# A second Strassen level for output product 4, with the sums behind h split at the chunk boundary

## The chip, the core and the metric

The kernel runs on one core of a Trainium2 chip. A core has a matrix engine (TensorE, PE in the profile; its weight loads are listed as PEld), a vector engine (VectorE, DVE), a scalar engine (ScalarE, ACT), a general engine (GpSimd, POOL) and SyncE (SP), which here only issues DMAs. Each engine works through its own instructions in order and waits on semaphores where it needs another engine. Matmul results land in PSUM, which has eight banks of 2 KB per partition; everything else lives in SBUF. The metric is the device time of one execution in microseconds (us). It is a little longer than the span of the profile, which runs from the first to the last instruction.

## The reference

All data are float32. A linear attention feeds a two-layer network:

```python
def _attn_ref(q, k, v, g_norm):            # (8, 8, 576, 64) each
    kv = np.einsum('bhsd,bhse->bhde', k, v)
    out = np.einsum('bhsd,bhde->bhse', q, kv)
    rms = np.sqrt(np.mean(out * out, axis=-1, keepdims=True) + 1e-06)
    return (out / rms * g_norm).astype(np.float32)

def _moe_ref(x, w_in, w_out):              # (4608, 512), (512, 2048), (2048, 512)
    h = x @ w_in
    g = np.maximum(0.01 * h, h)
    return (g @ w_out).astype(np.float32)
```

The attention's output is turned to (4608, 512) before it goes into the network. The two products of the network are nearly all of the arithmetic.

## The kernel before

**Blocks and chunks.** The 4608 rows are nine blocks of 512 (`NB`), the 2048 hidden columns four chunks of 512 (`NC`). Block 0 is computed plainly while the weights arrive. Blocks 1 to 8 use the Strassen-Winograd scheme: a product of 2x2 blocks from seven products instead of eight, at the price of sums of operands and of results. The products are numbered 1 to 7 and run in the order 1, 2, 6, 5, 7, 3, 4 (`ORDER`). In what follows h1 means product 1 of the hidden layer, o4 product 4 of the output. The output chunks are counted through as n = 4 (block - 1) + chunk, from 0 to 31.

**The hidden product.** From block 2 on h is computed by two levels (`product_h_two`, L930): each outer product holds seven inner ones of 128 columns each. Outer group k runs 7 matmuls in two PSUM banks, four in one and three in the other (`ha` and `hb`, or `hc` and `hd`). ACT copies the first results of a quadrant to `qa` and `qc` in SBUF, and DVE adds the later ones. At the end of a chunk seven DVE adds of 512 columns each turn `qa` and `qc` into g's four quadrants (L959 to 967), ACT applies the leaky ReLU (`relu`), and POOL forms the four operand sums of the output product (`sums_of`). h4 of the chunk is the last before that; h1 of the next chunk overwrites the first part of `qa` and `qc`.

**The output product.** `product_o` (L973) runs one product per slot, each four matmuls of 256 columns into a bank `oa` or `oc`. A chunk has seven slots, t = 0 to 6; in each, PE does one group of h and then one output product of an earlier chunk. o1 of chunk n begins in slot 2 of the following chunk. A bank keeps accumulating: 1, 6, 7, 4 in one, 2 in the other, then 5 and 3 in that other one again. After each product DVE (ACT for the first writing of a block) adds the bank into one of four output tiles, named `11`, `12`, `21`, `22`. From chunk 4 on product 2 is itself done by a second level: its seven matmuls of 128 columns use the fourth column group that the three-product bank of h leaves empty (`Second`, L905); there the order is 1, 5, 6, none, 7, 3, 4. Its operand sums of g come from POOL (`inner_g`, L893), 128 columns each.

**Right-hand sides.** The sums of w_out's blocks are formed once, in block 1, by POOL (`sides_w2`), written to DRAM, and from then on loaded by SP for each chunk into `t12` (products 5 and 6) and `t34` (products 7 and 4), 512 KB each. w_in's 49 pieces per chunk are read group by group into a ring of five (`read`, `RING`).

**Order.** From block 2 on the order on each engine is the program's (`pin`). The loop near the end of the function places attention work of the next batch (`FINE_SLOTS`, `LATE_SLOTS`) and the x sums of the next block (`sides_x`, slots 20 to 22, with POOL's `inner` in slots 24, 25 and after 27) into the slots, counted 0 to 27 within a block.

Of the kernel before, what the change touches and what calls it, by code (L numbers as in the profile page):

```python
# [23 lines left out]
def kernel(  # L24
# [77 lines left out]
    pairs = consts.tile([P, 4 * NW], F32, name="pairs")  # L102
# [85 lines left out]
    ident = consts.tile([P, P], F32, name="ident")  # L188
# [470 lines left out]
    t12, t34 = pair(2, 2, U, N2), pair(3, 2, U, N2)  # L659
    writes = []  # L660

    def sides_w2(n):
# [7 lines left out]
        def sums(i):  # L670
            t = (t12, t34)[i]
            if n >= NC:
                pin(nc.sync.dma_start(t, w2_dram[c][i]))
                return
# [73 lines left out]
    xt24 = [work.tile([P, 2, 2, N2], F32, tag="xt24", name="xt24"),  # L748
# [3 lines left out]
    def sides_x(i):  # L752
# [7 lines left out]
        if i == 1:  # L760
            t4 = opool.tile([P, 2, N2], F32, tag="o", name="xt4", bufs=6)
# [22 lines left out]
        def inner(kind):  # L784
            for y11, y12, y21, y22, t1, t2, t4 in batches:
# [10 lines left out]
    def strassen(tags, left, right, done, order=ORDER, pieces=None):  # L796
# [4 lines left out]
        for i in order:  # L801
# [21 lines left out]
            for part in range(2):  # L823
                for r in range(2):
                    matmul(bank[:, part, :], lhsT=left(i, part, r), rhs=right(i, part, r),
                           start=i in FRESH and part == 0 and r == 0, stop=(r == 1),
                           skip_group_check=True)
            done(i, bank.rearrange("p u (v n) -> p (u v) n", v=2))
            yield

    def relu(t, src=None):
        nc.scalar.activation(t, t if src is None else src, func=AF.Prelu, alpha=SLOPE)  # L832
# [48 lines left out]
    gi = view(pairs, 12 * P, 4, P)  # L881
# [11 lines left out]
    def inner_g(c, half):  # L893

        g = g_of(c)[3]
        a11, a21, a12, a22 = (g[:, n, :] for n in range(4))
        s1, s2, s3, s4 = (gi[:, n, :] for n in range(4))
# [31 lines left out]

    def product_h_two(i, c, quarters, to, second):  # L930
# [5 lines left out]
        banks = {}  # L936
        for t, k in enumerate(ORDER):
            for js, tags, q in zip(GROUPS, (("ha", "hc"), ("hb", "hd")), (qa, qc)):
# [11 lines left out]
                if fresh:  # L950
                    nc.scalar.copy(q[:, at], bank)  # L951
                else:
                    add(nc.vector, q[:, at], bank, q[:, at])
# [4 lines left out]
        g11, g21, g22, g12 = g_of(c)  # L958
        add(nc.vector, g21, qa[:, :, 0, :], qa[:, :, 1, :])  # L959
        add(nc.vector, g11, qa[:, :, 0, :], qc[:, :, 0, :])  # L960
        yield
        add(nc.vector, g22, g21, qa[:, :, 2, :])
        add(nc.vector, g12, g22, qa[:, :, 3, :])
        yield
        add(nc.vector, g22, g22, qc[:, :, 1, :])
        yield
        add(nc.vector, g21, g21, qc[:, :, 1, :])
        add(nc.vector, g21, g21, qc[:, :, 2, :])
        for t in (g11, g12, g22, g21):
            relu(t)  # L970
        sums_of(c, to)

    def product_o(n, g_sides, os, finish, second):  # L973
# [3 lines left out]
        sums = sides_w2(n + 1)[1] if n + 1 < NC * (NB - 1) else lambda i: None  # L977
        if c == 0:

            for key in ("12", "22", "11", "21"):  # L980
                os[key] = opool.tile([P, 2, N2], F32, tag="o", name=f"o{key}", bufs=6)

# [6 lines left out]
        def done(i, bank):  # L989
            key, fresh = into[i]  # L990
            if isinstance(bank, list):
# [13 lines left out]
            if c == NC - 1 and i in (2, 7, 3, 4):  # L1005
                finish(key, os[key])

            if i == (6 if second else 5):
                sums(0)
            elif i == 4:  # L1010
                sums(1)


        yield from strassen((("oa", "oc"), ("oc", "oa"))[n % 2], lambda i, part, r: g_sides[i][:, 2 * r + part, :],
                            lambda i, part, r: w_sides[i][:, r, :], done,
                           (1, 5, 6, None, 7, 3, 4) if second else ORDER,
                           pieces=pieces)
# [19 lines left out]
    def first_block(between):  # L1037
# [28 lines left out]
        for t in range(4):  # L1066
            o = opool.tile([P, DM], F32, tag="o", name="o", bufs=6)
# [47 lines left out]
    LATE_SLOTS = (3, 4)  # L1115

# [6 lines left out]
    seconds = {}  # L1123
# [12 lines left out]
    for i in range(1, NB):  # L1136
# [4 lines left out]
        for c in range(NC):  # L1141
# [3 lines left out]
            for t in range(7):  # L1145
                slot = 7 * c + t
                go(h_steps, 1)
                if not one:

                    if t == 6:  # L1150
                        go(h_steps, 1)
                    if slot in LATE_SLOTS:
# [102 lines left out]
```

## Time and profile before

| what | value |
|---|---|
| median of 3 runs | 917.1 us (916.8 to 918.18) |
| the profiled execution's own time | 917.21 us |
| its span | 915.5 us |
| granted TensorE clock | 1.00 |
| POOL, four sums of g per output chunk (128x512) | 1277 to 1376 ns each |
| POOL, operand sum of product 2 (128x128) | 456 to 510 ns each |
| DVE, add of an output bank (128x512) | 683 ns |
| DVE, add of a product-2 result (128x128) | 286 ns |
| DVE, add for g (128x512) | 684 to 692 ns |
| SP, load of t12 or t34 (512 KB) | 4.3 us from issue to landing |

A row of the profile gives a source line, an engine, an operation, the tile written and the tiles read, shapes, a count, busy time, the mean duration and the idle time before it with what ended it. Many rows have one helper's line: L118 is the matmul helper and L636 the add helper, so tiles tell them apart. A float32 matmul shows as two records. Durations of matmuls overlap, so their cost is read from start to start.

### The profile page before, as it was taken

The page shows a single profiled execution, that of the slowest core. Times are in us where ns is not written, and L with a number is a line of the kernel's source. Part 1 is how long each engine was busy: PE and PEld are TensorE (multiplying, and loading weights), DVE is VectorE, ACT ScalarE, POOL GpSimd, SP SyncE. Part 2 cuts the span into 40 slices and gives each one's busy share as a digit, 9 for nine tenths or more (in the row PEclk, how much of TensorE's full clock was granted, in tenths as well). Part 3 has the DMA queues.
Part 4 walks back from the last instruction along what each step waited for, and adds up shares of the span by engine and source line. Part 5 has one row for each costly group of instructions (what it writes and reads, how often), then busy time and mean ns, then how long its engine had stood idle before and what let it go on. Part 6 is the DMA issues. An engine that isn't in the chain of part 4 may idle for free.

```text
span 915.5 us, 18030 instructions
## 1 busy us (share of the span) xinstructions
PE 909.1 (99%) x6976; PEld 775.6 (85%) x6976; DVE 628.2 (69%) x1168; ACT 327.6 (36%) x645; POOL 367.0 (40%) x440
## 2 busy tenths in 40 slices
PE   8999999999999999999999999999999999999998
PEld 5444448888998999899999999999999999999997
DVE  5876985587457876587756786678659755755565
ACT  5454533242135233533343324332343333223330
POOL 2000246977633472226321642264226422642222
DMA  9999908895599678877896689658765676667632
GB/s 267 243 243 237 239 35 258 263 304 167 175 360 286 224 213 263 235 233 211 255 261 216 219 250 263 230 179 227 224 184 176 188 221 200 184 187 223 199 107 92
DMA packets 90229, 200.06 MB, mean 219 GB/s; under 512 B 9888, under 2 KB 42272, under 8 KB 90144
## 3 DMA queue, kind: packets, MB, share of 16 engines
q1 hardware_dynamic: 79680, 187.04, 69.5%
q10 hardware_dynamic: 10016, 10.69, 3.4%
q8 instruction: 56, 0.92, 0.4%
q0 software_dynamic: 448, 1.18, 0.3%
q14 instruction: 29, 0.24, 0.1%
HBM read 172.39 MB, written 26.48 MB: 217 GB/s over the span
## 4 chain that ended last, share of the span: by engine, by line
PE 95%; DMA 2%; DVE 1%; POOL 1%; issue 0%; ACT 0%; ACTq 0%; DVEq 0%; POOLq 0%
PE o_a L118 18%; PE o_c L118 18%; PE h_ha L118 11%; PE h_hb L118 11%; PE h_hc L118 8%; PE h_hd L118 8%; PE o_acc L118 6%; PE h_ps L118 6%; PE o_ps L118 3%; PE h_a L118 1%; PE h_c L118 1%; PE kv_ps L118 1%; DMA pairs<-in_v_dram 1%; PE h_b L118 1%; PE h_d L118 1%; DMA w<-pairs 1%
## 5 line engine op out<-in xcount | busy, mean ns | idle before, releaser
L636 POOL TENSOR_TENSOR gs<-g 128x512 f32<-128x512 f32 x64 | 81.7, 1277 | 253.3 <-ACT g L832 253.3
L832 ACT ACTIVATE g<-g 128x512 f32<-128x512 f32 x124 | 78.2, 631 | 130.4 <-DVE g L636 130.4
L951 ACT COPY w_all<-h_ha 128x512 f32<-128x512 f32 x84 | 48.9, 582 | 173.9 <-PE h_ha L118 160.5
L118 PE MATMUL o_a<-pairs,gs 128*128 128x256 f32 x384 | 91.3, 381 | 0.0
L118 PE MATMUL o_c<-pairs,gs 128*128 128x256 f32 x376 | 89.2, 380 | 0.0
L636 DVE TENSOR_TENSOR o<-h_hb,o 128x128 f32<-128x128 f32 x104 | 29.8, 286 | 83.3 <-ACT pairs L951 83.2
L118 PEld LDWEIGHTS o_a<-pairs,gs 128*128 128x128 f32 x384 | 69.8, 190 | 9.2 <-POOL pairs L636 1.2
L636 DVE TENSOR_TENSOR o<-o_c,o 128x512 f32<-128x512 f32 (+1 forms) x91 | 61.1, 672 | 24.1 <-PE o_c L118 23.7
L118 PEld LDWEIGHTS o_c<-pairs,gs 128*128 128x128 f32 x376 | 68.3, 190 | 7.6
L636 DVE TENSOR_TENSOR o<-o_a,o 128x512 f32<-128x512 f32 x75 | 51.2, 682 | 28.2 <-PE o_a L118 28.1
L118 PE MATMUL h_ha<-stage,w_all 128*128 128x128 f32 x448 | 59.6, 276 | 0.0
L118 PEld LDWEIGHTS h_ha<-stage,w_all 128*128 128x128 f32 x448 | 56.6, 192 | 3.0 <-issue 0.7
L118 PE MATMUL h_ps<-xT,w_all 128*128 128x512 f32 (+1 forms) x136 | 58.1, 571 | 0.3 <-DVE w_all L258 0.3
L118 PE MATMUL o_acc<-w,g 128*128 128x512 f32 x128 | 57.7, 594 | 0.0
L636 DVE TENSOR_TENSOR g<-g,pairs 128x512 f32<-128x512 f32 x84 | 55.6, 689 | 1.9
L636 POOL TENSOR_TENSOR pairs<-g 128x128 f32<-128x128 f32 x52 | 23.7, 456 | 77.3 <-PE h_hb L118 48.5
L118 PEld LDWEIGHTS h_ps<-xT,w_all 128*128 128x128 f32 x136 | 25.4, 190 | 29.0 <-issue 26.1
L118 PEld LDWEIGHTS o_acc<-w,g 128*128 128x128 f32 x128 | 24.1, 190 | 30.2 <-issue 29.9
L636 DVE TENSOR_TENSOR w_all<-h_hc,w_all 128x512 f32<-128x512 f32 x56 | 38.3, 684 | 15.9 <-PE h_hc L118 15.6
L636 DVE TENSOR_TENSOR o<-h_hd,o 128x128 f32<-128x128 f32 x78 | 22.0, 283 | 38.2 <-ACT pairs L951 38.1
L118 PE MATMUL h_hb<-stage,w_all 128*128 128x128 f32 x336 | 46.7, 275 | 0.0
L636 POOL TENSOR_TENSOR pairs<-w 128x512 f32<-128x512 f32 x4 | 5.3, 1328 | 98.7 <-ACT cut L245 98.7
(229 smaller groups left out, 2262.4 us busy)
## 6 DMA issues: line engine op xcount, KB each, us to landing
w_all<-w SPq DMA_DIRECT2D x196, 448.0 KB, 4.2
pairs<-w SPq DMA_DIRECT2D x56, 512.0 KB, 4.3
out_dram<-o ACTq DMA_DIRECT2D x35, 256.0 KB, 4.4
v_in<-in_v_dram SPq DMA_DIRECT2D x29, 288.0 KB, 5.5
k_in<-in_k_dram SPq DMA_DIRECT2D x28, 288.0 KB, 5.3
q_in<-in_q_dram SPq DMA_DIRECT2D x56, 144.0 KB, 6.0
q_in<-in_q_dram SPq DMA_DIRECT2D x56, 140.0 KB, 6.0
w<-stage SPq DMA_DIRECT2D x12, 512.0 KB, 4.8
```

The costliest lines, as they stand in the source:

```text
L118: pin(nc.tensor.matmul(*args, **kw))
L636: ins = eng.tensor_tensor(out_, a, b_, op=ALU.subtract if minus else ALU.add)
L832: nc.scalar.activation(t, t if src is None else src, func=AF.Prelu, alpha=SLOPE)
L951: nc.scalar.copy(q[:, at], bank)
```

## The change

For the 21 chunks n = 8 to 28, product 4 is taken out of the sequence and done by two levels in a bank of its own use: seven matmuls of 128 columns in four steps, in slots 1 to 4 of the chunk after the one in which o1 ran (step 1 directly behind o1 of the next chunk). The bank is the one that held products 1, 6 and 7, after it was read. Its results go into tile `21` as seven parts of 128 columns. The sum of products 1, 6 and 7, which product 4 used to be added to, now goes into a tile `7` of its own, which is added to `22` and `21` once per block. The order of the other products becomes 1, none, 6, 5, 7, 3, none.

The operands: POOL's `inner_g` forms its sums for two quadrants of g at once (256 columns). Seven right-hand pieces per chunk are formed on POOL in block 2, written to DRAM by POOL's DMA queue (`w4_dram`), and loaded by SP from block 3 on (`f4` and `f4_more`); the load of `t34` is split accordingly.

The seven adds for g are split: first all seven for the quadrant that the next h1 overwrites (128 columns), then the rest (384 columns), two at once, two at the end of the chunk, and three after the next chunk's h1. The ReLUs, the copies of h and the sums of g follow in program order. The x sums move from slots 20 to 22 to slots 22, 24 and 25, POOL's `inner` parts are spread over slots 24, 25, 26 and the next block's slot 0. Output tiles are taken when first written, from four buffers and two for `11`, where there were six; `ident` moves into the home of `xt24`.

```diff
-    pairs = consts.tile([P, 4 * NW], F32, name="pairs")
+    pairs = consts.tile([P, 4 * NW + 4 * P], F32, name="pairs")
...
+    w4_dram = [dram.tile([P, 7, P], F32, name=f"w4_{c}") for c in range(NC)]
+    t12, t34 = pair(2, 2, U, N2), view(pairs, 28 * P, 2, U, N2)
+    f4 = t34[:, 1].rearrange("p u (v n) -> p (u v) n", v=2)
+    f4_more = view(stage, 21 * P, 3, P)
+
+    def four(n):
+        return 2 * NC <= n < NC * (NB - 1) - 3
...
+            if n >= NC and i:
+                if row != 1:
+                    pin(nc.sync.dma_start(t[:, 0], w2_dram[c][i][:, 0]))
+                if row == 0:
+                    return
+                if not four(n):
+                    pin(nc.sync.dma_start(t[:, 1], w2_dram[c][i][:, 1]))
+                    return
+                pin(nc.sync.dma_start(f4, w4_dram[c][:, :4, :]))
+                pin(nc.sync.dma_start(f4_more, w4_dram[c][:, 4:, :]))
+                return
...
-        a11, a21, a12, a22 = (g[:, n, :] for n in range(4))
-        s1, s2, s3, s4 = (gi[:, n, :] for n in range(4))
+        a11, a21, a12, a22 = (g[:, n, 2:, :] for n in range(4))
+        s1, s2, s3, s4 = (gi_two[:, :, n * P:n * P + P] for n in range(4))
...
+    class Fourth:
+        STEPS = (1, 2, 5), (6, 3), (7,), (4,)
+        COLUMN = {1: 0, 6: 0, 7: 0, 4: 0, 2: 1, 5: 2, 3: 2}
...
+        def step(self, at):
+            if at == 0:
+                self.bank = ps_m.tile([P, 4, P], F32, tag=self.tag, name=f"f_{self.tag}")
+            for k in self.STEPS[at]:
+                matmul(self.bank[:, self.COLUMN[k], :], lhsT=self.left[k], rhs=self.right[k],
+                       start=(k == 1), stop=True, skip_group_check=True)
+            for k in self.STEPS[at]:
+                bank = self.bank[:, self.COLUMN[k], :]
+                v, s = INTO[k]
+                to = self.o_of("21")[:, v, s * P:s * P + P]
+                if self.n % NC == 0 and k in (1, 5, 6, 4):
+                    nc.scalar.copy(to, bank)
+                else:
+                    add(nc.vector, to, bank, to)
+            if at == 3:
+                self.last()
...
+        for _ in add_up(0, 1):
+            pass
+        for _ in add_up(1, 4):
+            yield
         yield
-        for t in (g11, g12, g22, g21):
-            relu(t)
+        for g in g_of(c):
+            pin(relu(g))
         sums_of(c, to)
...
+            if fourth and i == 7:
+                if c == NC - 1 or not four(n + 1):
+                    add(nc.vector, os["22"], os["22"], os["7"])
+                if c == NC - 1:
+                    finish("22", os["22"])
...
+            elif i == 4 and NC <= n < 2 * NC:
+                inner_w4()
+                pin(nc.gpsimd.dma_start(w4_dram[c][:, :4, :], f4))
+                pin(nc.gpsimd.dma_start(w4_dram[c][:, 4:, :], f4_more))
+                later.append([3, lambda: sums(1, 1)])
...
+        def last():
+            sums(1, 1)
+            if c == NC - 1 or not four(n + 1):
+                add(nc.vector, os["21"], os["21"], os["7"])
+            if c == NC - 1:
+                finish("21", os["21"])
+        order = ORDER
+        if fourth or four(n - 1):
+            order = (1, None, 6, 5, 7, 3, None if fourth else 4)
...
+    FOURTH_AT = {1: 0, 3: 2, 4: 3}
...
+                    if t == 0:
+                        go(h_rest)
+                    if slot == 0 and inner_rest:
+                        inner_rest(2)
+                    if t in FOURTH_AT and four((i - 1) * NC + c - 2):
+                        fourths[(i - 1) * NC + c - 2].step(FOURTH_AT[t])
...
-                        if slot in (20, 21, 22):
-                            go(sums, 2 if slot == 20 else 1)
+                        if slot in (22, 24, 25):
+                            go(sums, 2 if slot == 24 else 1)
                         if slot == 24:
-                            inner(0)
+                            inner(0, (1, 3))
                         elif slot == 25:
-                            inner(1)
+                            inner(0, (0,))
+                            inner(1, (0, 3))
+                        elif slot == 26:
+                            inner(0, (2,))
+                            inner(1, (1, 2))
...
-            go(h_steps)
+            if one or (i, c) == (NB - 1, NC - 1):
+                go(h_steps)
+            else:
+                go(h_steps, 1)
+                h_rest = h_steps
```

`add_up(lo, hi)` holds the seven adds of before for the quadrants lo to hi; `inner_w4` forms the three sums and the difference of the right-hand pieces by four POOL instructions of 128 columns.

## The prediction

> **What bounds the kernel now.** I read the page's busy shares first, then the chain of waits, then the wait list of the tensor engine alone, then the table of stretches for one block of 512 rows, and last the timelines of each engine around one chunk.
>
> ```profile
> PE 909.1 (99%) x6976; PEld 775.6 (85%) x6976; DVE 628.2 (69%) x1168; ACT 327.6 (36%) x645; POOL 367.0 (40%) x440
> ...
> PE 95%; DMA 2%; DVE 1%; POOL 1%; issue 0%; ACT 0%; ACTq 0%; DVEq 0%; POOLq 0%
> ```
>
> The wait list of PE (who waited, on whom, us in total, times, longest), and the stretch of one block (its length, then busy us and instructions of PE, PEld, DVE, ACT and POOL, clock, DMA share, GB/s):
>
> ```profile
> PE idle_ps L118 <- DVE group L294: 1.5, 1, 1.5
> PE kv_ps L118 <- DMA pairs<-in_v_dram: 0.8, 1, 0.8
> ...
> 446.17:543.05 96.88, 96.88 (x849) 89.86 (x848) 69.72 (x135) 35.51 (x72) 38.12 (x48) 1.00 0.79 237
> ```
>
> To be seen: TensorE (PE) is the bound, 95% of the chain. Its two longest waits, 1.5 and 0.8 us, lie in the start. In the block from 446.17 to 543.05 it is busy for all 96.88 us at full clock, while VectorE (DVE) is busy 72%, ScalarE (ACT) 37%, GpSimd (POOL) 39% and the DMA engines 79%. So time falls only with PE's own work, and rises only where PE starts to wait. What a product costs is read from PE's timeline (start, us, engine, line, operation, tiles, count):
>
> ```profile
> 513.16 1.89 PE L118 MATMUL o_a<-pairs,gs 128*128 128x256 f32 x8
> 514.89 0.38 PE L118 MATMUL h_hc<-xT,w_all 128*128 128x128 f32 x2
> ...
> 516.67 1.06 PE L118 MATMUL h_ha<-stage,w_all 128*128 128x128 f32 x8
> ```
>
> From start to start, four matmuls of 256 columns (each is two records) take 514.89 - 513.16 = 1.73 us. The next eight of 128 columns take 516.67 - 514.89 = 1.78 us, 0.2225 each. The durations beside them overlap and are not used.
>
> **What the Trainium skill says.** "SBUF — State Buffer", section "Who interferes with whom": a DVE instruction with two SBUF inputs and a GpSimd instruction that reads SBUF take the same port, and the second blocks for the other's whole length. The trace agrees: DVE's x subtraction takes 0.68 us with POOL idle and 1.28 us beside one of POOL's sums:
>
> ```profile
> 495.55 0.68 DVE L636 TENSOR_TENSOR w_all<-xT 128x512 f32<-128x512 f32 x1
> 502.27 1.28 DVE L636 TENSOR_TENSOR xT<-xT 128x512 f32<-128x512 f32 x1
> ...
> 501.74 1.26 POOL L636 TENSOR_TENSOR gs<-g 128x512 f32<-128x512 f32 x1 [9.38 <-ACT g L832]
> 503.08 1.62 POOL L636 TENSOR_TENSOR gs<-gs,g 128x512 f32<-128x512 f32 x1
> ```
>
> "PSUM — Partial Sum Buffer", section "PSUM bank collisions raise a hardware error": two engines on one bank must be ordered, readers too. Here that shows as DVE's 128x128 add waiting for ACT's copy from the same bank:
>
> ```profile
> 532.71 0.48 ACT L951 COPY pairs<-h_hd 128x384 f32<-128x384 f32 x1 [0.31 <-PE h_hd L118]
> ...
> 533.22 0.29 DVE L636 TENSOR_TENSOR o<-h_hd,o 128x128 f32<-128x128 f32 x1 [1.29 <-ACT pairs L951]
> ```
>
> "DMA: Bandwidth & Descriptors", section "Anatomy of one DMA — SWDGE (gpsimd) path", prices a GpSimd DMA at 2.0 us plus bytes at 436 GB/s: about 2.6 us for 256 KB. The trace shows such DMAs only in the crowded start.
>
> **The change part by part.** The clock of one chunk, from its first h matmul, in us of PE time: h1 0, o3 of the chunk before 1.78, h2 3.51, step 0 of the new product 5.29, h6 5.96, o1 7.74, step 1 9.47, h5 9.91, step 2 11.69, h7 11.92, step 3 13.70, o6 13.92, h3 15.65, o5 17.43, h4 19.16, o7 20.94, end 22.67. A tile is readable about 0.25 us after its last issue (ACT's copies start 0.3 us after it).
>
> 1. Matmuls. 21 chunks (n = 8 to 28) replace 1.73 us by 7 x 0.2225 = 1.56 us: 0.17 each, 21 x 0.1725 = 3.6 us off PE. It is all on the path. The built order has 147 of the new matmuls, 21 x 7, and no other PE work changes.
>
> 2. Evacuation. One add of 512 (next one starts 0.60 after) becomes seven of 128 (0.20 apart, 0.29 where one needs the other). Splitting g turns 7 adds into 7 of 128 and 7 of 384 (0.47 apart): 7 x 0.68 against 7 x 0.60, +0.6. About +1.6 us of DVE per chunk of 22.7, in a lane with some 6 us free: no cost in total, only where a column is needed back. Steps 0 to 3 reuse column 0, so each waits for the evacuation before it. Tightest is step 2 to step 3: h5 is readable at 11.94, ACT's copy ends at 12.45, the 128x128 add of the same bank follows, then step 2's own add, done at about 13.05; step 3 wants it at 13.70. Spare 0.65. The cover is h7; without it every chunk would stall by over 1 us.
>
> 3. g split. DVE's quadrant adds run from -0.8 to 1.0, the rest from 1.0 to 5.3; ACT's relus now stand behind h1's copies and end near 7; POOL's s1 starts at 6.5 and s2 ends at 9.1. o1 (7.74) needs only g11, o6 (13.92) needs s2: spare over 4. h6 needs h1's bank back: before that copy came at +4.4 (499.52), now at 2.5. No cost.
>
> 4. POOL. Four operand sums double from 128 to 256 columns (456 to about 750 ns, from the 128x256 rows): +1.2 us per chunk, POOL about 45% busy. But in the last chunk of a block the inner x sums now wait for x terms that DVE makes at about 17.6 (they moved from slots 20 to 22 to slots 22, 24, 25). After that POOL still has some 8.7 us of work (twelve sums, 0.46 to 0.76 each) and ends about 2 us inside the next chunk; before, it ended at 518.57, ahead of g's adds. There the quadrant adds share its port: a 128x128 SBUF add beside POOL is 548 ns in the block-1 rows, so 7 of them take about 3.1 us and not 1.8. With the two 1.25 us q transposes of slots 1 and 2 (1.08 apart) ahead, step 1's evacuation ends near 12.0; step 2 wants it at 11.69. Stall about 0.3, at the start of blocks 4, 5 and 6 (later ones have no q left): 0.9 us. Bounds: 0 if POOL ends early, 0.6 each if DVE loses the port throughout.
>
> 5. Last chunk of a block. With attention, x terms and step 3's add, DVE frees step 3's bank at about 19.1; o5 wants it at 19.6 (PE has 2.2 us of attention there). Spare 0.2 to 0.5 in five blocks. I take 0.1 in all, bounds 0 and 1.5.
>
> 6. DMA. Per chunk 256 KB become 448 KB: 21 x 192 KB, 4 MB on 200. Loads go out at 13.9 and are used 14 us later; they land in 4.3 us. SP holds them until step 3 is done, and behind them stand the reads of w1's ring, each free 17 us ahead: nothing. In block 2 POOL forms the sums (4 x 0.46) and writes them out by its own queue four times. Write, wait and reload must fit in seven slots, about 24.7 us: POOL is done at 13.7, the write lands by 17 (skill's price) to 22 (8 us, the start's POOL rows), the reload 4.3 later, before 28.1. Only the third write has 2.7 us more POOL work before it and could be late. Bounds 0 and 2 us; I take 0.
>
> 7. Moved homes (ident, output tiles) and ACT's copies at a block's first chunk: all released a chunk or more before use, nothing. The three last chunks keep the old product; g11's relu comes by 894, o1 wants it at 900.06: nothing.
>
> Sum on the profiled execution's 917.2 us (span 915.5): -3.6 + 0.9 + 0.1 = -2.6, so 914.6. It lies 0.1 above the median of 917.1, which changes nothing. Beyond 0.2% (1.8 us, what a measurement can tell from no change): under 915.3 is faster, over 918.9 slower.
>
> **The rivals.**
> - B, the gain is mostly eaten. For: the port and the bank of points 4 and 5, with spares below 0.5 us that come from a schedule added up by hand. Against: each occurs once per block. Price: 3 x 0.6 + 5 x 0.2 = 2.8 plus some of point 6: -0.8 or so, 916.4.
> - C, slower: the column 0 chain in step 1 to step 3. If one attention operation of 1.1 to 1.25 us stands ahead of an evacuation on DVE or ACT in each of the 14 chunks that carry attention (10 to 23), the evacuation is 1.2 late, the spare 0.65 is gone and PE waits 0.6: 14 x 0.6 = 8.4, less 3.6 is +4.8, 922. It decides for slower from 5.4 / 14 = 0.39 us a chunk, that is, from 1.04 us later than in point 2. Against: in the built order these operations stand behind step 2's add, except in the first chunk (point 4).
> - That the change does nothing is ruled out by the 147 matmuls; more than 3.6 us cannot come, as PE has no waits to lose in the loop.
>
> **How the numbers follow.** Likeliest, A: 914.6, own range 913.4 (all of 3.6, no stall) to 915.3, chance 0.65. B, 0.22, from 915.3 to 918.9. C, 0.13. The range 913.4 to 917.6 leaves out C and the upper end of B. Faster 0.65, same 0.22, slower 0.13.
>
> **What would show it.** Right: 147 matmuls f<- of 0.22 us start to start; the chunk on PE shorter by 0.17; in PE's wait list at most single waits of 0.3 us on DVE, at blocks 4 to 6's first chunks; POOL busy up to 2 us past a block's start. Wrong: f or o matmuls waiting for DVE in most chunks (C), or for a DMA in the second block (point 6).

## The result, and the profile after

| kernel | median | runs | lowest to highest |
|---|---|---|---|
| before | 916.72 us | 6 | 916.44 to 918.18 |
| changed | 921.25 us | 6 | 920.52 to 923.01 |

The ratio is 1.0049, 95% interval [1.0037, 1.0062]: slower by 4.5 us, where 914.6 was forecast, with a range from 913.4 to 917.6. The profiled execution of the changed kernel took 920.52 us with a span of 918.8, so 3.3 us over the profile before. It is the fastest of its six.

The page, busy time of the engines and the chain of waits:

```profile
PE 908.7 (99%) x7102; PEld 776.6 (85%) x7102; DVE 678.7 (74%) x1478; ACT 330.1 (36%) x669; POOL 417.9 (45%) x464
...
PE 88%; DVE 5%; POOL 3%; DMA 2%; issue 1%; ACT 1%; DVEq 0%; ACTq 0%; SPq 0%; POOLq 0%
```

PE has 126 records more and 0.4 us less busy time. The forecast's 3.6 cannot be read there, as the page counts a stall as busy in part (block 5's first chunk: 23.40 of 23.93 us busy, with some 1.2 of stall). PE's share of the chain fell from 95% to 88%, and DVE and POOL took 5% and 3%. PE's wait list (us in total, times, longest):

```profile
PE idle_ps L118 <- DVE group L295: 1.5, 1, 1.5
PE o_a L118 <- issue: 1.4, 1, 1.4
PE f_oa L118 <- DVE o L637: 1.2, 3, 0.4
PE o_c L118 <- DVE o L637: 0.8, 1, 0.8
PE h_ha L118 <- ACT w_all L1029: 0.5, 1, 0.5
```

The first wait is the old one of the start. The other four are new. The `f_oa` row is the forecast's own sign, three waits of 0.4 at three blocks' starts. The `o_a`, `o_c` and `h_ha` rows were not forecast. The stretch of the block that was shown before, from and to the same h1:

```profile
448.06:545.52 97.46, 96.93 (x873) 90.11 (x872) 77.78 (x185) 36.02 (x76) 44.26 (x48) 1.00 0.77 243
```

It has become longer, 97.46 for 96.88 us, and PE is no longer busy in all of it. The whole difference lies in a few chunks. A chunk is written here as the block whose rows h is computed for, and its place in it. Lengths from h1 to h1, read from PE's timeline of the two kernels, in us:

| chunk | before | changed | difference |
|---|---|---|---|
| all others from n = 10 on, for instance block 5's third | 25.19 | 25.02 | -0.16 to -0.17 each |
| block 2's last, block 3's first | 24.27, 22.86 | 24.40, 24.59 | +0.13, +1.73 |
| block 4's, 5's, 6's first | 22.87, 22.86, 22.87 | 23.88, 23.93, 24.09 | +1.01, +1.07, +1.22 |
| block 6's last | 24.08 | 24.54 | +0.46 |
| block 7's, 8's first | 22.87, 22.87 | 23.02, 22.88 | +0.15, +0.01 |
| block 7's last | 23.26 | 22.70 | -0.56 |
| last h4 to the end | 27.6 | 28.6 | +1.0 |

With 0.165 us saved in each of 21 chunks, the matmuls give 3.5 us, as forecast. Against them stand stalls of 1.86 us (block 3), 3.80 (blocks 4 to 6: the difference and 0.165, each), 0.48 (blocks 7 and 8), 0.63 (block 6's end) and 1.0 (tail), less 0.40 for a stall of the kernel before in block 7 that is gone. The sum is +3.9; the profiled start was 0.65 us shorter, which makes the 3.3.

**Where a block begins.** DVE, POOL and PE of the changed kernel around h1 of block 5 (521.59), from the timeline:

```profile
521.07 0.72 POOL L637 TENSOR_TENSOR w_all<-w_all 128x256 f32<-128x256 f32 x1
521.66 0.28 DVE L637 TENSOR_TENSOR g<-w_all 128x128 f32<-128x128 f32 x1
521.75 0.77 POOL L637 TENSOR_TENSOR pairs<-g 128x256 f32<-128x256 f32 x1
521.87 0.81 DVE L637 TENSOR_TENSOR g<-w_all,pairs 128x128 f32<-128x128 f32 x1
522.49 0.78 POOL L637 TENSOR_TENSOR pairs<-g,pairs 128x256 f32<-128x256 f32 x1
522.60 1.14 DVE L637 TENSOR_TENSOR g<-g,w_all 128x128 f32<-128x128 f32 x2
523.77 0.82 DVE L637 TENSOR_TENSOR g<-g,pairs 128x128 f32<-128x128 f32 x3
...
528.83 0.68 DVE L637 TENSOR_TENSOR o<-o_c,o 128x512 f32<-128x512 f32 x1
529.12 0.39 PE L118 MATMUL h_hb<-w,pairs 128*128 128x128 f32 x2
529.66 1.97 PE L118 MATMUL o_c<-w,g 128*128 128x256 f32 x8
...
532.70 1.23 DVE L456 STREAM_TRANSPOSE qT<-q_in 128x576 f32<-128x576 f32 x1
533.77 0.60 DVE L637 TENSOR_TENSOR o<-f_oa,o 128x128 f32<-128x128 f32 x2
534.43 0.49 PE L118 MATMUL f_oa<-stage,pairs 128*128 128x128 f32 x2 [0.39 <-DVE o L637]
```

The seven quadrant adds run from 521.66 to 524.51, 2.85 us. In the tail, where POOL is idle, the same seven take 1.79 (892.95 to 894.74). Until POOL ends at 523.27, one 128x128 add occupies up to 0.81 us and not 0.28. All that DVE does next is late. o3's evacuation ends at 529.51 and lets o1 into its bank at 529.66, while h6 had been issued by 529.34 (529.12 and 0.22). These 0.32 us cost 0.57 in all, as o1 takes 1.89 us to the next start and not 1.73, and the first matmul of step 1 0.32 and not 0.22. Step 1's two adds, behind a q transpose, end at 534.37; step 2 follows, 0.55 us late, at a cost of 0.66. The two make the 1.24 us of this chunk.

The adds that are lengthened have both inputs in SBUF. A DVE add of a PSUM bank is not: in block 2's last chunk, at 319.53, one of 128x512 takes 0.68 us beside POOL's 128x128 sum from 319.56, which takes 0.46.

In block 3 it is worse, as POOL also forms block 2's `inner_w2` sums:

```profile
327.40 1.55 DVE L637 TENSOR_TENSOR g<-g,w_all 128x128 f32<-128x128 f32 x2
328.98 1.70 DVE L637 TENSOR_TENSOR g<-g,pairs 128x128 f32<-128x128 f32 x3
...
330.96 0.76 POOL L637 TENSOR_TENSOR w<-w,w 128x128 f32<-128x128 f32 x1
332.06 0.68 DVE L637 TENSOR_TENSOR o<-o_a,o 128x512 f32<-128x512 f32 x1
332.84 1.97 PE L118 MATMUL o_a<-pairs,g 128*128 128x256 f32 x8 [1.38 <-issue]
```

POOL works to 331.7, the seven adds take 4.1 us (326.46 to 330.60), o7's evacuation starts at 332.06, and o4, of the last chunk that still has the old product 4, waits for it. The wait is listed under "issue", but PE goes on 0.1 us after that evacuation ends.

### The profile page after: what moved, and what is told of

Read it like the earlier page. It is cut to its first block, busy times and chain, and to the rows that moved or that the text cites. A ratio compares the mean times of both kernels' runs of the same rounds, so it can differ in the third digit from the quotient of the medians.

```text
span 918.8 us, 18822 instructions
## 1 busy us (share of the span) xinstructions
PE 908.7 (99%) x7102; PEld 776.6 (85%) x7102; DVE 678.7 (74%) x1478; ACT 330.1 (36%) x669; POOL 417.9 (45%) x464
## 4 chain that ended last, share of the span: by engine, by line
PE 88%; DVE 5%; POOL 3%; DMA 2%; issue 1%; ACT 1%; DVEq 0%; ACTq 0%; SPq 0%; POOLq 0%
PE o_a L118 15%; PE o_c L118 14%; PE h_ha L118 10%; PE h_hb L118 10%; PE h_hc L118 7%; PE h_hd L118 7%; PE o_acc L118 6%; PE h_ps L118 6%; PE o_ps L118 3%; PE f_oa L118 2%; PE f_oc L118 2%; PE h_a L118 2%; PE h_b L118 1%; DVE o L637 1%; PE h_c L118 1%; PE h_d L118 1%
## 5 line engine op out<-in xcount | busy, mean ns | idle before, releaser
L853 ACT ACTIVATE g<-g 128x512 f32<-128x512 f32 x124 | 72.1, 624 | 95.1 <-DVE g L637 95.0
L637 DVE TENSOR_TENSOR g<-g,pairs 128x128 f32<-128x128 f32 (+1 forms) x168 | 67.7, 430 | 2.9
L637 DVE TENSOR_TENSOR o<-o_c,o 128x512 f32<-128x512 f32 (+1 forms) x81 | 54.1, 667 | 20.2 <-PE o_c L118 20.1
L637 DVE TENSOR_TENSOR o<-o_a,o 128x512 f32<-128x512 f32 x64 | 43.7, 683 | 23.1 <-PE o_a L118 23.0
L637 DVE TENSOR_TENSOR g<-g,w_all 128x128 f32<-128x128 f32 (+1 forms) x112 | 50.7, 452 | 2.0
L637 POOL TENSOR_TENSOR pairs<-g 128x256 f32<-128x256 f32 x52 | 41.7, 801 | 18.1 <-PE h_hb L118 13.9
L1029 ACT COPY pairs<-h_hb 128x384 f32<-128x384 f32 x84 | 40.4, 481 | 16.0 <-PE h_hb L118 12.6
```

The source lines that it names most:

```text
L637: ins = eng.tensor_tensor(out_, a, b_, op=ALU.subtract if minus else ALU.add)
L853: return nc.scalar.activation(t, t if src is None else src, func=AF.Prelu, alpha=SLOPE)
L1029: pin(nc.scalar.copy(q[:, at], bank))
```

## The experiments

The theory: POOL's work, pushed past the block's end, holds the SBUF port while DVE adds up the first quadrant, and the evacuations behind are late. Rivals: the q transposes; the order of the adds; the new product's own evacuations; the moved tiles. In the tables each median stands beside that of the kernel before on the same chip, and "chunks" are lengths from h1 to h1 against the changed kernel. All diffs are against the changed kernel unless said.

**The x sums back in their old slots.**

```diff
-                        if slot in (22, 24, 25):
-                            go(sums, 2 if slot == 24 else 1)
+                        if slot in (20, 21, 22):
+                            go(sums, 2 if slot == 20 else 1)
...
-                            inner(0, (1, 3))
+                            inner(0)
...
-                    inner_rest = inner
+                inner(2)
```

> The x sums on DVE go back to slots 20, 21 and 22 and POOL's twelve inner sums back to slots 24, 25 and the block's end; all else is the changed kernel. Port theory (POOL's work, pushed past the block's end, holds the port while DVE adds up the first quadrant): POOL is done before those adds, the seven take 1.8 us again and not 2.9 to 4.1, and the stalls at the starts of blocks 3 to 8 (1.9 + 3.8 + 0.5 us) mostly go: 4 to 6 us off 921.3, so 915.3 to 917.3. Rival, the two q transposes at slots 1 and 2 alone make step 1 late: at most 1 us off, 920.3 or more. Rival, the order of adds (first quadrant ahead of the output's evacuations) is enough by itself: no change, 921.3.

927.92 us, before 917.17, ratio 1.0119 [1.0106, 1.0132]. None of the three expectations held. The first chunks of blocks 4 to 7 did get 0.3 to 0.5 us shorter, but those of blocks 3 and 8 0.6 and 1.3 longer, and blocks 3 to 5 lost 1.0 to 1.1 us in their last chunk and block 6 3.3. There the four x sums stand on DVE ahead of an evacuation of the new product: PE's wait list has 4.4 us in four waits of `f_oc` for DVE. The longest, 2.03 us in block 6, was followed by 3.4 us at half clock, which is why block 6 lost so much more. And the port was not free: four inner sums now ran directly ahead of the block's start and on into it, and the quadrant adds took 3.3 us. So this run doesn't test the port; it shows that the x sums could not stay where they were.

**The q transposes later.**

```diff
-    FINE_SLOTS = {1: 1, 2: 1, 4: 1, 9: 1, ...
+    FINE_SLOTS = {3: 1, 5: 1, 6: 1, 9: 1, ...
```

> The first three q transposes of a block stand at slots 3, 5 and 6 and not at 1, 2 and 4; all else is the changed kernel. Port theory: the part of the stall that lies at o1 (0.5 to 0.75 us in each of blocks 4, 5 and 6) and all of block 3's stay, the part at step 2 (some 0.66 us each) goes: about 2.0 us off 921.3, 919.3. Rival, the transposes are the whole cause: 3.8 us off, 917.5. Rival, the order of adds: no change.

930.83 us, before 917.17, ratio 1.0142 [1.0128, 1.0157]. At the starts of blocks 4, 5 and 6 the expected happened, 0.66, 0.68 and 0.67 us shorter, all of it at step 2. But block 2's second chunk became 7.0 us longer and block 3's 1.9: PE waits 4.09 us in block 2 for `v_in`, whose loads are queued by the step that holds the transpose, and 1.61 in block 3 for a piece of w_in (`w_all`).

**The last chunk's g whole.**

```diff
+        if (i, c) == (NB - 1, NC - 1):
+            for _ in add_up(0, 4):
+                yield
```

> In the last chunk of all, g is added up by seven adds of 512 columns as in the kernel before; all else is the changed kernel. If the tail's 0.96 us (o5 of the last but one product waits for DVE, which has the first quadrant's seven adds and two more ahead) comes from the split: 1.0 us off, 920.3, and nothing else in the trace changes. Rival, it comes from the evacuations that were late before it: no change, 921.3. The port has no part in it, POOL is idle there.

920.53 us, before 917.17, ratio 1.0040 [1.0028, 1.0052]. From the last h4 to the end 27.5 us and not 28.6; every other chunk within 0.03. The median is 3.4 us over the kernel before on its chip, where the changed kernel was 4.5 over; the spread of the runs (919.1 to 922.43) is wider than the effect, so it is the trace that shows it. The changed kernel's tail, and then this one's:

```profile
894.00 0.82 DVE L637 TENSOR_TENSOR g<-g,pairs 128x128 f32<-128x128 f32 x3
...
895.68 0.68 DVE L637 TENSOR_TENSOR o<-o_c,o 128x512 f32<-128x512 f32 x1
896.41 1.78 PE L118 MATMUL o_c<-pairs,gs 128*128 128x256 f32 x7 [0.81 <-DVE o L637]
```

```profile
892.62 0.68 DVE L637 TENSOR_TENSOR g<-w_all 128x512 f32<-128x512 f32 x1
893.22 0.69 DVE L637 TENSOR_TENSOR g<-w_all,pairs 128x512 f32<-128x512 f32 x1
893.83 0.68 DVE L637 TENSOR_TENSOR o<-o_c,o 128x512 f32<-128x512 f32 x1
```

Ahead of the evacuation that o5 waits for stand nine adds in the first, two in the second.

**The moves without the product.**

```diff
     def four(n):
-        return 2 * NC <= n < NC * (NB - 1) - 3
+        return False
```

> The second level of product 4 is left out (its four matmuls of 256 columns and one evacuation as in the kernel before, no third sums or their transfers); the moved x sums, the moved inner sums, the doubled operand sums on POOL and the split g stay. PE has 3.6 us more than the changed kernel. Port theory: the waits at o1 at the block starts stay (1.4 us in block 3, some 1.9 in blocks 4 to 6), those at step 2 go as there is no step 2, the tail's 1.0 stays: 921.3 + 3.6 - 2.0 = about 922.5 to 923. Rival, the new product's own seven evacuations per chunk are what makes DVE late: the stalls go with it and the time is the one before or up to 1 us over it, 916.7 to 918.

921.50 us, before 917.17, ratio 1.0054 [1.0041, 1.0068]. The moves alone cost; the rival's 918 falls. But not at o1, as expected: the blocks' first chunks are within 0.3 us of the kernel before, so the stalls there went with the product, as the rival had it. In block 3 the seven adds still take 3.85 us beside POOL, but they begin 0.04 us ahead of h1 and not 0.57 behind it; in blocks 4 to 6, where h1 itself is late, they take 2.2 to 2.3 us, and no step 2 stands behind them. POOL's work beside the adds thus costs PE time only where something behind them is due soon. The tail has its wait as before (1.3 us over the kernel before, with the split of g still there). The other waits lie at the end of the last chunks of blocks 3 to 6 (0.2 to 0.9 us over the kernel before), where h1 waits for ScalarE's copy of h4, behind two `spread` copies, behind a reciprocal that is late on DVE. That is the wait the changed kernel has at the end of block 6 only.

**POOL's inner sums left out.** This kernel leaves out the twelve inner sums for the x of each block from block 3 on; the products read what lies there.

```diff
-                        if slot == 24:
-                            inner(0, (1, 3))
...
-                else:
-                    inner_rest = inner
```

> From block 3 on POOL's twelve inner sums of the next block's x are left out (their products read what lies there); all else is the changed kernel. Port theory: POOL is done before the first quadrant's adds at the starts of blocks 4 to 7, the seven take 1.8 us and not 2.9 and more, and the stalls there (1.2 + 1.2 + 1.4 + 0.3 us) go nearly whole, of block 3's 1.7 some 0.7: 4 to 5 us off 921.3, so 916.3 to 917.3. Order theory (with the split g, nine adds and not two stand ahead of the evacuations of o7 and o3 on DVE, and this suffices): the stalls stay, 921.3.

917.02 us over 22 runs, before 916.94, ratio 0.9998 [0.9986, 1.0010]. First chunks of blocks 3 to 8 shorter by 1.62, 0.75, 0.66, 0.72, 0.21 and 0.17, block 6's last by 0.27: 4.4 us (block 2's and 5's last are 0.27 and 0.10 longer), at the size that the port theory gave, though in block 3 more and in blocks 4 to 6 less. The seven adds at block 5's start took 1.79 us. What stays in blocks 4 to 6 (0.43 to 0.67 us) is at step 2.

**The adds behind o7's evacuation.**

```diff
-                    if t == 6:
-                        go(h_steps, 1)
...
                 elif waited == LAG:
                     go_o()
...
+                if t == 6 and not one:
+                    go(h_steps, 1)
```

> The first quadrant's seven adds and the first two of the rest are put on DVE behind the evacuation of o7, not ahead of it; all else is the changed kernel. Order theory: block 3's wait of 1.4 us (o4 after o7 in one bank) goes, the tail's 0.8 goes too if the wait there is for an evacuation that stands behind these nine adds; the starts of blocks 4 to 6 gain little, as o3's evacuation still stands behind all of g's adds: 2.0 us off, 919.3. Port theory alone: DVE has the same work beside the same POOL work, every wait stays: 921.3.

924.71 us, before 916.94, ratio 1.0078 [1.0057, 1.0100]. Block 3's wait of 1.38 us, o4 for o7's evacuation, went, and o1, one product later, waited 1.06 us: the chunk became 0.12 us shorter. In the tail o5's wait of 0.81 went, and the product behind it waited 1.76 (`o_a` in the wait list), so that the tail became 0.9 us longer. The second chunks of blocks 4 to 8 got 0.38 us longer each, where DVE first idles 0.9 us for o7, then has all of g ahead of o3's evacuation, and o1 waits for that; in the last chunks of blocks 4 to 6 a step of the new product waits, 0.66 each. The order decides, but in both directions: whichever stands behind is late. The expected 919.3 fell.

**Only the moved homes, and the kernel before again.** The diff is against the kernel before.

```diff
-    pairs = consts.tile([P, 4 * NW], F32, name="pairs")
+    pairs = consts.tile([P, 4 * NW + 4 * P], F32, name="pairs")
...
-    ident = consts.tile([P, P], F32, name="ident")
+    ident = xt24_home[:, 0, 0, :P]
```

> The kernel before with only the homes moved: ident in the x sums' tile, pairs longer by 512 words a partition and the second operand sums there, outputs in pools of four and two, four unused 448 KB tensors in DRAM. In the changed kernel and in all its variants the loads of the first 40 us ran at 202 to 221 GB/s between 20 and 40 us and the queue was 3 to 6 us late, in the kernel before at 244 GB/s. Homes theory (where the tiles lie makes the loads slower): 205 to 220 GB/s here too, and 0 to 4 us added, some 918.5. Rival (the rate is chance, or comes from something else in the program, its length for one): 240 GB/s and 917.2.

> The kernel before, for a second trace of its start. If 244 GB/s between 20 and 40 us is its own, that is seen again, and the loads of weights at 34 to 46 us go out as early as in the first trace (34.2 and 45.5 us); if it is chance, some 210 GB/s. 917.2 us either way, as PE waits for none of them.

917.44 us over 20 runs, before 916.94, ratio 1.0002 [0.9993, 1.0011]. The loads ran at 220 GB/s between 20 and 40 us here, and at 208 in the second trace of the kernel before (916.98 us). The slower loads thus come without the change too, and nothing ties them to it.

**POOL's work moved, none left out.**

```diff
+        if held:
+            pin(nc.gpsimd.tensor_copy(mark[:1], g_of(c)[1][:1, 3, :1]))
+            inner_g(held.pop(), 1)
...
+                            if half and c == NC - 1 and i + 1 < NB:
+                                held.append((now - 1) % NC)
+                            else:
+                                inner_g((now - 1) % NC, half)
-                    if t == 5 and now <= 2 * NC:
+                    if t == (2 if c == NC - 1 else 5) and now <= 2 * NC:
```

> Two pieces of POOL's work leave the block's end; all else is the changed kernel. Second half of the inner g sums in a block's last chunk (1.5 us) now waits for the last of DVE's g adds; block 2's last four inner w2 sums (2 us) stand three slots earlier. Port theory: in blocks 4 to 6 POOL ends at about the first quadrant's first add, the seven take 1.8 to 2.0 us, 0.7 us less stall each, 0.2 each in blocks 7 and 8; block 3, where 5 us of POOL's work reach past the boundary and 3.5 leave, 0.7 to 1.5 less: 3 to 4 us off 921.3, 917.3 to 918.3. If leaving out the inner sums had helped for another reason than the port, 921 or so.

916.12 us over 13 runs, before 916.36, ratio 0.9999 [0.9991, 1.0007]: 5 us off, a little more than expected. First chunks of blocks 3 to 8 shorter by 1.11, 1.07, 1.08, 1.10, 0.22 and 0.18. The timeline at block 5's start (h1 at 521.82), DVE and POOL:

```profile
521.27 0.73 POOL L637 TENSOR_TENSOR w_all<-w_all 128x256 f32<-128x256 f32 x1
521.87 0.28 DVE L637 TENSOR_TENSOR g<-w_all 128x128 f32<-128x128 f32 x1
522.07 0.28 DVE L637 TENSOR_TENSOR g<-w_all,pairs 128x128 f32<-128x128 f32 x1
522.27 0.61 DVE L637 TENSOR_TENSOR g<-g,w_all 128x128 f32<-128x128 f32 x2
522.92 0.82 DVE L637 TENSOR_TENSOR g<-g,pairs 128x128 f32<-128x128 f32 x3
523.65 0.55 DVE L637 TENSOR_TENSOR g<-w_all 128x384 f32<-128x384 f32 x1
...
528.13 0.17 POOL L1044 COPY mark<-g 1x1 f32<-1x1 f32 x1 [6.13 <-DVE g L637]
```

POOL's two 256-column sums are out of the way, behind the one-element copy that waits for DVE's last add, and the seven adds take 1.78 us. Nothing else differs there from the changed kernel. This shows that POOL's two sums beside the adds made them long. That the two meet at a port is the prediction's reading, which these times fit and no run shows by itself.

**The q transpose behind step 1, in every block, then from block 4 on.** The second diff moves it for `i > 3` alone.

```diff
-                    for _ in range(FINE_SLOTS.get(slot, 0)):
+                    for _ in range(FINE_SLOTS.get(slot, 0) if slot != 2 else 0):
...
+                if slot == 2 and not one:
+                    go(a_steps, 1)
```

> The q transpose of slot 2 stands on DVE behind step 1's evacuations, not ahead of them; all else is the changed kernel. If the part of the stall at step 2 (0.4 to 0.66 us in each of blocks 4, 5 and 6) is that 1.1 us transpose: it goes, 1.3 to 2.0 us off 921.3, 919.3 to 920, and the part at o1 stays. Against the earlier run with three transposes later, the loads of later inputs are not delayed, as the transpose moves by 0.6 us only. Rival, step 1 is late from the queue ahead of it alone: no gain.

> The q transpose of slot 2 stands behind step 1's evacuations from block 4 on only; in blocks 2 and 3, where a transpose is followed by more loads, it stays; all else is the changed kernel. If the loss of the run that moved it everywhere lay in those loads: no wait at the second chunks of blocks 2 and 3, 0.65 us less stall at step 2 in each of blocks 4, 5 and 6, so 2.0 us off 921.3, 919.3. If DVE or another queue pays for the move: less than 1 us off.

Everywhere: 924.28 us, before 916.36, ratio 1.0089 [1.0076, 1.0102]. From block 4 on: 919.47 over 21 runs, before 917.29, ratio 1.0033 [1.0019, 1.0047]. In both, blocks 4, 5 and 6 lost 0.65 to 0.68 us of stall each. In the first, block 2's second chunk took 4.4 us more and block 3's 2.1, in the second neither did. So DVE pays nothing that shows for the move from block 4 on, and the 919.3 expected there held. The loss in block 2 is a load's: one is queued per slot, so a slot's delay in the step that orders them sent a `v_in` load out at 260.47 and not at 255.72, and PE waited 2.52 us for it. In block 3 PE waits 1.84 us for ScalarE's copy of a bank of h, and ScalarE had stood still for 4.13 us before that copy, behind an output store; what the transpose has to do with that is open.

**g not split at all.**

```diff
-        for _ in add_up(0, 1):
-            pass
-        for _ in add_up(1, 4):
+        for _ in add_up(0, 4):
...
-                go(h_steps, 1)
-                h_rest = h_steps
+            go(h_steps)
```

> g is added up whole by seven adds of 512 columns, two before o7's evacuation and the rest at the chunk's end, as in the kernel before; the second level of product 4, the moved sums and POOL's doubled operand sums stay. Theory that the split itself (nine adds ahead of o7's evacuation) costs the time: block 3's 1.4 us and the tail's 1.0 go, and some of the 0.5 to 0.75 at o1: 3 us off, 918.3. Theory that the split is needed (h1's copies wait for the quadrant's last add, now at 4.4 us and not at 2.5, and with POOL at work later still; h6 wants h1's bank, step 0 its place on DVE): every chunk may wait, 0.2 us or more each, 5 us on, 926.

949.73 us, before 916.36, ratio 1.0361 [1.0348, 1.0375]. The split is needed, far more than the expected 926 had it. Of PE's waits the longest in total is now:

```profile
PE h_ha L118 <- ACT w_all L1029: 22.2, 18, 2.6
```

h6 wants h1's bank, whose ScalarE copies stand behind all of g. In the order before, h6 came 1.06 us later in the chunk: o4's 1.73 us stood where step 0's 0.67 now stand.

**The fixes together.** First POOL's two pieces, the transpose everywhere and the last chunk's whole adds; then the same with the transpose from block 4 on; then with `inner_w2` a chunk earlier and block 6's spread copies behind h4:

```diff
+                    if (slot, i) == (27, 6):
+                        go(a_steps, 1)
...
+                    if now == 2 * NC - 2 and t == 2:
+                        inner_w2(2)
```

> The last chunk's whole adds, POOL's two moved pieces and the q transpose behind step 1, together on the changed kernel. If the three causes add up: 1.0 + 3.5 + 1.6 us off 921.3, some 915.2, which is 1.8 us under the kernel before, PE's wait list holding no wait over 0.3 us after 230 us but block 3's rest and the 0.6 at the end of block 6. If they are one cause seen three times, 917 to 918.

> POOL's two moved pieces, the q transpose behind step 1 from block 4 on, and the last chunk's whole adds, on the changed kernel. If the three causes add up: 916.1 (POOL's pieces alone) less 0.5 (what is left at step 2 of blocks 4 to 6: 0.11, 0.15, 0.29) less 1.0 (tail) is 914.6, some 1.8 us under the kernel before. If the tail's or the transpose's part is chance: 915.6 to 916.1.

> As three_fixes, and block 2's last four inner w2 sums on POOL stand a whole chunk earlier, and in block 6 DVE's reciprocal and ScalarE's two spread copies stand behind the last h evacuation and not ahead of it. If block 3's rest (0.8 us) is POOL's work past the boundary and the end of block 6 (0.6 us) is those copies: 1.2 to 1.4 us under three_fixes, some 913.3, which is the kernel before less the 3.6 us of matmuls. If the copies only move the wait to h6 of block 7: 914.

| fixes | median | runs | before | ratio |
|---|---|---|---|---|
| three, transpose everywhere | 922.82 us | 6 | 916.36 us | 1.0067 [1.0050, 1.0083] |
| three, transpose from block 4 | 915.42 us | 21 | 917.29 us | 0.9972 [0.9962, 0.9983] |
| five | 915.06 us | 21 | 917.29 us | 0.9977 [0.9963, 0.9990] |

The first missed its 915.2 by what the transpose brings everywhere: 4.2 and 4.3 us in the second chunks of blocks 2 and 3. The second and third are faster than the kernel before by 1.9 and 2.2 us, and not told apart from each other. The second's 915.42 lies 0.8 over what was expected of the sum; its trace has each of the three parts, with 22.70 us in the first chunks of blocks 4 to 6 and 27.5 from the last h4 to the end. With five, the first chunks of blocks 4 to 8 take 22.70 or 22.71 us (22.87 before), block 6's last 23.91 (24.08), block 3's first 22.97 (22.86), and the end 27.5. The stalls named in the table above are gone in blocks 4 to 8 and in the tail, each by its own edit. Block 3's is not: its first chunk became shorter by what block 2's last became longer, 47.95 us for the two with five fixes, 47.75 with three and 47.13 before. What is new is 0.23 us in block 7's second chunk and 0.6 at the end of block 2, which the run with only the transpose moved from block 4 on shows as well (24.98 us), though nothing of block 2 is edited there. PE's wait list with five fixes:

```profile
PE kv_ps L118 <- DMA v_in<-in_v_dram: 1.6, 1, 1.6
PE idle_ps L118 <- DVE group L295: 1.5, 1, 1.5
PE kv_ps L118 <- DMA pairs<-in_v_dram: 0.7, 1, 0.7
PE h_ha L118 <- ACT w_all L1031: 0.5, 1, 0.5
```

The three longest are the start's; the last is at the end of block 2. Its cause can be read in the timeline, DVE and POOL in block 2's last chunk:

```profile
318.85 1.52 DVE L637 TENSOR_TENSOR w_all<-xT,w_all 128x512 f32<-128x512 f32 x1
319.08 0.74 POOL L637 TENSOR_TENSOR stage<-xT 128x256 f32<-128x256 f32 x1
```

It is again an add with two SBUF inputs beside a sum of POOL, an x sum this time. In the changed kernel the same two took 0.94 and 1.27 us, so that POOL was held for longer; in the run with only the transpose moved from block 4 on, 1.51 and 0.74. DVE's began first by 0.22 to 0.25 us in all three: the order of the starts in the trace does not tell which one is held, where the prediction had "the second blocks for the other's whole length". DVE's 0.6 us are then missing ahead of the reciprocal, ScalarE's `spread` copies and its copy of h4, the path of block 6's end. So which engine is held can differ between kernels whose order there is the same, and a stall with it. The expected 913.3 was reached in the lowest runs (913.02 and 913.41) and not in the median. Whether the changed start has longer waits more often than the one before is not settled; the kernel before had runs up to 922.99 too.

## Why the prediction was wrong

The forecast of 914.6 failed at its term 4, which had 0.9 us for 3.8 and nothing for block 3's 1.9 and the 0.5 of blocks 7 and 8, and at term 7, which had nothing for the tail's 1.0. Term 5 was 0.6 and not 0.1. Terms 1, 2, 3 and 6 stand.

- **1, matmuls, 3.6 us off.** Held: 21 chunks by 0.165 are 3.5.
- **2, the column-0 chain, spare 0.65.** Held. No undisturbed chunk stalls, and rival C, a stall in each of the 14 chunks with attention, did not occur; that the time came out near its 922 is chance, as it came from other places.
- **3, split g at no cost.** Held for the three consumers that it named (o1, o6, h6). Without the split the kernel is over 28 us slower. What was missed is the evacuation of o7 and o3, which the split puts behind nine adds; that counts under 4 and 7.
- **4, "Stall about 0.3, at the start of blocks 4, 5 and 6", 0.9 us.** This step failed, by size. Its mechanism is what the runs showed: POOL ended 1.7 us inside the chunk (2 was forecast), the seven adds took 2.85 us (3.1). But the stalls are 1.18, 1.24 and 1.38 us, 3.8 in sum. Lateness was followed to one consumer, step 2, and DVE's queue was summed about 1 us too short: even with the port free (POOL's work moved) step 1's evacuation ends 11.7 us into the chunk, where the forecast had 12.0 with the port's 1.3 in it. And o3's evacuation, which stands behind the same adds, was not followed at all: o1's wait for it costs 0.57. The bounds of 0 to 0.6 a block left that out.
- **4 again, which blocks.** "The start of blocks 4, 5 and 6" was chosen for the q transposes. The port needs none: block 3 lost 1.86 us, as in block 2 POOL has `inner_w2` and `inner_w4` besides, and blocks 7 and 8 lost 0.5. Block 3's adds also begin later, 0.57 us behind h1 and not 0.07 as in block 5, and o4 is due soon behind them. Block 3's part of POOL's work was summed for the round trip of point 6 only, as a deadline of POOL's writes and not as an occupation of the port.
- **5, last chunk of a block, 0.1.** Spare was enough in four of the five blocks; block 6's end lost 0.63 through a path that was not in the list (DVE's reciprocal, ScalarE's copies ahead of h4's). Bounds 0 and 1.5 held it.
- **6, DMA at nothing.** Held: no wait on the new loads. The round trip had room, with 4.8 and 4.9 us for POOL's two kinds of writes (median), where the Trainium skill's "Anatomy of one DMA — SWDGE (gpsimd) path" in "DMA: Bandwidth & Descriptors" gives an estimate of 2.6 and 2.5; the measured times decide.
- **7, "The three last chunks keep the old product [...] nothing".** Wrong by 1.0 us. The check was made on g11's ReLU for o1, but the adds' new order holds up o2's evacuation, which o5 needs (0.81 us of wait, gone with whole adds).

The Trainium skill's "SBUF — State Buffer", section "Who interferes with whom", was the right page: it has a DVE instruction with two SBUF inputs and a GpSimd instruction that reads SBUF in each other's way. One of this case's traces has the same adds beside POOL and without it, 2.85 and 1.79 us, and an experiment that moved POOL's work alone has 1.78.

## What to carry to other kernels

A delay on an in-order engine is to be followed to every consumer behind it in the built order, and not only to the one that was looked for: here seven short adds, 1.1 us late, held up o3's evacuation and step 1's, and through them o1 and step 2. Work that is moved to get out of one engine's way lands beside something; ask what the moved work now runs beside, and what its issue orders, loads too. A change that loses may still hold its gain: three small reorderings turned 4.5 us of loss into 1.9 of gain.

## What the runs showed of the hardware

Some waits of PE cost more than their length. In the run with the transpose moved everywhere, PE waited for a load at 263.8, from PE's timeline:

```profile
266.35 0.96 PE L118 MATMUL kv_ps<-v_in,k_in 64*64 64x64 f32 x29 [2.52 <-DMA v_in<-in_v_dram]
```

The stretches around and after it (length, then busy us of PE, PEld, DVE, ACT and POOL, the granted clock, DMA share, GB/s):

```profile
264.00:267.00 3.00, 0.65 (x29) 0.66 (x32) 0.00 (x0) 0.09 (x1) 2.54 (x6) 0.93 1.04 413
267.00:270.00 3.00, 3.00 (x56) 2.61 (x51) 0.00 (x0) 0.00 (x0) 0.00 (x0) 0.50 1.05 388
270.00:273.00 3.00, 3.00 (x22) 2.82 (x22) 0.88 (x2) 0.58 (x1) 0.00 (x0) 1.00 0.96 375
```

The clock was granted at half for 3.4 us from 266.6 on, and the chunk became 4.41 us longer for a wait of 2.52.

The traces have nine such stretches, behind waits of 1.85 to 4.09 us; each lasts 3.4 us at half clock, the one behind the longest 6.8. Seven of the waits were for `v_in` ahead of the small matmuls of `kv_ps`. The other two were not: 2.03 us for an evacuation of the new product (x sums in their old slots, half clock from 709.7 to 713.1) and 2.22 for a copy of h (three fixes with the transpose everywhere, from 369.7 on). No wait of 1.84 us or less had one behind it, as the 1.38 us in block 3 of the changed kernel. But a longer wait need not: the trace of the kernel without the split has five from 1.89 to 2.64 us before h6 and stays at 1.00, while its other five runs have a mean granted clock of 0.992 to 0.996. So the length of the wait counts, and it does not decide alone; what else does is open.

Waits for loads in the first 120 us come in some executions and not in others. Of the fourteen traces of the changed kernel and its variants, seven have one of 1.27 to 3.03 us for `v_in` at 70 to 92 us, the other seven none. The kernel before has none in its two traces, but 7 of its 58 runs in the last comparison have a mean clock of 0.996 to 0.998, and they take 919.8 to 923.0 us. The rate of loads differs too with the same program: its second trace had 208 GB/s between 20 and 40 us where the first had 244.
